# Spreading the first triangular inverse of a delta-rule kernel by four row masks instead of two, with a share of it on GpSimd

## The chip, the cores and the metric

The kernel runs on one core of one Trainium2 chip. The metric is the device time of one execution in microseconds (us). The kernel before takes 661.8 us, the median of 3 runs (661.51 to 662.65). One execution more was taken with the hardware profiler on; all instants below are counted from the start of its span.

## The reference, cut to what matters

Two blocks follow each other. The first is a delta rule over 4 batches x 8 heads, 768 steps, head size 48:

```python
k_n = k / (np.linalg.norm(k, axis=-1, keepdims=True) + 1e-06)
for t in range(S):
    kt, vt, bt = (k_n[:, :, t], v[:, :, t], beta[:, :, t, None])
    y[:, :, t] = np.einsum('bhd,bhde->bhe', q[:, :, t], state)
    v_old = np.einsum('bhde,bhd->bhe', state, kt)
    state = state + bt[:, :, :, None] * np.einsum('bhd,bhe->bhde', kt, vt - v_old)
```

The second is a SwiGLU feed-forward block on its output, 3072 tokens of 384 values, with 1536 hidden units:

```python
g = x @ w_gate
silu = g * (1.0 / (1.0 + np.exp(-g)))
val = x @ w_val
return (silu * val @ w_out)
```

## The kernel before, in words

**Chunks.** The 768 steps are cut into 12 chunks of C = 64 steps. Inside a chunk the recurrence is a triangular system: with A the lower part of the keys' Gram matrix, scaled by beta, the chunk needs Z = (1 + A)^-1. Two chunks form a group. 32 matrices (two chunks x 16, the 16 being "heads of a batch pair") of a group lie side by side in the lanes of VectorE. For the groups after the first, Z is made in 32 x 32 blocks; for the first group, which nothing can hide, it is made in 16 x 16 blocks only (B16 = 16, R = 32), and the parts below these blocks are brought in by matmuls.

**The first group, around the change.**
- `first_tiles` (line 606) clears the place of Z (`first_of["zb"]`, 1056 columns) and makes row masks from the identity: each `tensor_reduce` (line 619) sums some columns of it in both halves, so that a mask is 1 in certain partitions of each half of 64 and 0 elsewhere. `m_rows` holds four masks (rows from 16 on, from 32 on, from 48 on, and below 32), `m_low` the first three negated.
- `first_gram` (line 635) makes the Gram matrices in PSUM, chunk 0 in `px`, chunk 1 in the feed-forward banks 2 and 3. `first_diag` (line 645) puts their blocks on the diagonal into a tile; ScalarE does this for one half of the rows (line 650), VectorE adds the other (line 654). A transposition on VectorE (line 1950) turns "steps in partitions" into "matrices in partitions".
- `low_copies` (line 663) is six ScalarE instructions for a chunk (line 667): they copy the part of the Gram matrix below the blocks from PSUM into `l_sb`, negated and masked.
- `first_scale` (line 673) scales the blocks by beta over the squared norm; GpSimd writes that factor onto Z's diagonal (line 676), VectorE scales both blocks whole (line 680).
- `first_substitution` (line 689) is 15 steps of two VectorE instructions, a product (line 700) and a sum (line 706).
- `first_z` (line 708) transposes Z back on VectorE (line 710): 1024 columns, in rows of 32, of which half hold the 16 x 16 blocks' second half for the other mask.
- `spread_z` (line 713) writes Z into `ztp[0]`, where it serves as the weights of matmuls: one mask for the upper 32 rows, one for the lower 32. For chunk 0 it is four instructions of 256 columns, one on ScalarE (line 723) and three on VectorE (line 725); for chunk 1 it is one of 512 columns on each of the two.
- `n_products` (line 727) multiplies Z and the lower part: 64 matmuls of 64 x 64 (line 733) for a chunk, into banks 2 and 3. It needs all of `spread_z` for its chunk and all of `low_copies`. `first_advance` (line 940) begins with it, and its other products (line 952) follow, each on the one before, until x of chunk 0 is there (lines 1040 and 1041) and the feed-forward matmuls begin (line 1562).
- `unread` (line 630) is a filler: matmuls of a constant whose result nobody reads (line 633).

**What sets the order.** All five engines are under a manual schedule: each executes its instructions in the order in which the program text issues them, and waits in that order. So the end of the start phase is written out by hand at lines 1930 to 1990.

**The weights** come in pieces (`pieces`, numbered n). `stage(n, after)` (line 253) starts the DMA of a piece on SyncE's queue (line 262). With `after` given, GpSimd first copies one column from the staged piece `after` into the place of piece n (line 261): GpSimd thus waits until that earlier piece has landed, and SyncE waits for GpSimd, so that only a few pieces are on the way at once. Pieces 0 to 5 are staged right after `first_scale`, pieces 2 to 5 with `after` = 0 to 3. Later in GpSimd's order come the two halves of a mask on the products of q and k of chunk 0 (`under_mask`, line 537) and then the copies for pieces 6, 7 and so on.

Of the kernel before, what the change touches and what calls it, by code (L numbers as in the profile page):

```python
# [20 lines left out]
def kernel(  # L21
# [25 lines left out]
    nc = tc.nc  # L47
# [4 lines left out]
    NB = B // 2  # L52
# [5 lines left out]
    HH = NB * H  # L58
# [3 lines left out]
    const = ctx.enter_context(tc.tile_pool(name="const", bufs=1))  # L62
# [60 lines left out]
    ztp = [const.tile([128, 2, HH, C], FP32, name=f"zt{i}") for i in range(ZB)]  # L123
# [55 lines left out]
    def load_v(c):  # L179
        vin[c] = work.tile([128, 2, NB, NJ, D], FP32, name="vin", bufs=2)  # L180
        for b in range(2):
            src = halves(v, c, b).rearrange("bp (j par) p d -> par p (bp j) d", par=2)
            for par in range(2):
                s = half_of(b ^ par if c > 1 else b).start
                nc.sync.dma_start(  # L185
                    out=vin[c][s : s + 64, par].rearrange("p bp j d -> p (bp j) d"),
                    in_=src[par],
                )
# [28 lines left out]
    staged, powers, places = {}, {}, {}  # L217

    def words(tile_):
# [3 lines left out]
    places = {  # L223
        "z0": zt_flat[0],
        "z1": zt_flat[1],
        "wo": words(wo_sb).rearrange("p t d -> p (t d)"),
    }
    H_ = PIECE
# [12 lines left out]
    for n, (name, lo) in enumerate(place_of):  # L241
        m = 2 * pieces[n][4]
# [7 lines left out]
        at = max(before) if before else LATE.get(name, -1)  # L250
# [78 lines left out]
    for b in range(2):  # L329
        rows = mask_q[64 * b : 64 * b + 64]  # L330
        nc.gpsimd.affine_select(
            out=rows,
# [5 lines left out]
            channel_multiplier=-1,  # L338
        )

    m_rows = const.tile([128, 4], FP32, name="m_rows")
    m_low = const.tile([128, 3], FP32, name="m_low")
    m_two = const.tile([128, 4, 2], FP32, name="m_two")

    p_places = [const.tile([128, 1024], FP32, name=f"p_sb{i}") for i in range(2)]
    spent, late_loads = [], []
# [105 lines left out]
    def banks(name, tag):  # L452

        if type(tag) is int:
            return [ps_ffn([128, 512], name, tag + i) for i in range(2)]
        p = ps_pair(name, tag)
        return [p[:, 0], p[:, 1]]
# [100 lines left out]
    def new_mb():  # L558
        return work.tile([128, R, R], FP32, name="mb", bufs=1)
# [38 lines left out]
    first_of, l_sb, n_sb = {}, {}, {}  # L598
    B16 = R // 2

    def pairs_of_blocks(flat):

        v = flat.rearrange("p (b n) -> p b n", b=2)[:, :, 0 : B16 * R]
        return v.rearrange("p b (k i) -> p b k i", i=R)

    def first_tiles():
        a = work.tile([128, C * 2 * HH], FP32, name="a_sb")
        for c in range(2):
            l_sb[c] = a[:, R * R * c : R * R * (c + 1)].rearrange(
                "p (h k) -> p h k", k=C  # L610
            )
        first_of["flat"] = new_mb().rearrange("p k i -> p (k i)")
        first_of["zb"] = places["z1"].bitcast(FP32)[:, 4 * H_ - 1056 : 4 * H_]
        first_of["mb"] = places["wo"].bitcast(FP32)[:, 2 * H_ : 2 * H_ + 1056]
        nc.vector.memset(first_of["zb"], 0.0)
        for c in range(2):
            nc.vector.memset(l_sb[c][:, :, 48:C], 0.0)
        for x, rows in enumerate((slice(16, C), slice(R, C), slice(48, C), slice(0, R))):
            nc.vector.tensor_reduce(
                out=m_two[:, x],  # L620
                in_=ident.rearrange("p (b n) -> p b n", b=2)[:, :, rows],
                axis=mybir.AxisListType.X,
                op=ALU.add,
            )
        nc.vector.tensor_tensor(
            out=m_rows, in0=m_two[:, :, 0], in1=m_two[:, :, 1], op=ALU.add
        )
        nc.vector.tensor_scalar_mul(m_low, m_rows[:, 0:3], -1.0)

    def unread(count, p, m=512):  # L630

        for _ in range(count):
            nc.tensor.matmul(p[0:R, 0:m], half, half[:, 0:1].to_broadcast([128, m]))
# [11 lines left out]
    def first_diag(c, p, between=None):  # L645
        to = first_of["flat"].rearrange("p (j c par h) -> p c par j h", c=2, par=2, j=R)
        to = to[:, c]
        p = [p_h.rearrange("p x h j -> p x j h") for p_h in p]
        for par in range(2):
            nc.scalar.mul(to[:, par], p[par][:, 0], m_rows[:, 3:4])  # L650
            if between and par == 0:
                between()
        for par in range(2):
            nc.vector.scalar_tensor_tensor(
                out=to[:, par],
                in0=p[par][:, 1],
                scalar=m_rows[:, 1:2],
                in1=to[:, par],
                op0=ALU.mult,
                op1=ALU.add,  # L660
            )

    def low_copies(c, p):
        l_v = l_sb[c].rearrange("p (par h) k -> p par h k", par=2)
        for par in range(2):
            for x in range(3):
                nc.scalar.mul(
                    l_v[:, par, :, B16 * x : B16 * x + B16],
                    p[par][:, x // 2, :, B16 * (x % 2) : B16 * (x % 2) + B16],
                    m_low[:, x : x + 1],  # L670
                )

    def first_scale(r_b):
        zb, b = first_of["zb"], beta_b[:, 0]
        nc.vector.tensor_tensor(out=b, in0=b, in1=r_b, op=ALU.mult)
        nc.gpsimd.tensor_copy(zb[:, 0 : R * R : R + 1], b)
        mb = pairs_of_blocks(first_of["mb"])[:, :, :, 0:B16]
        for x in range(2):
            at = slice(B16 * x, B16 * x + B16)
            nc.vector.scalar_tensor_tensor(  # L680
                out=mb[:, x],
                in0=mb[:, x],
                scalar=-1.0,
                in1=b[:, None, at].to_broadcast([128, B16, B16]),
                op0=ALU.mult,
                op1=ALU.mult,
            )

    def first_substitution():

        zb, mb = pairs_of_blocks(first_of["zb"]), pairs_of_blocks(first_of["mb"])
        for j in range(B16 - 1):
            m = B16 - 1 - j
            shape = [128, 2, m, j + 1]
            t_v = tmp_of[nc.vector][:, 0 : 2 * (j + 1) * m].rearrange(
                "p (b i k) -> p b i k", b=2, i=m
            )
            z_v = zb[:, :, j + 1 : B16, 0 : j + 1]
            m_v = mb[:, :, j : j + 1, j + 1 : B16].rearrange("p b o i -> p b i o")
            nc.vector.tensor_tensor(  # L700
                out=t_v,
                in0=zb[:, :, j : j + 1, 0 : j + 1].to_broadcast(shape),
                in1=m_v.to_broadcast(shape),
                op=ALU.mult,
            )
            nc.vector.tensor_tensor(out=z_v, in0=z_v, in1=t_v, op=ALU.add)

    def first_z():
        z = new_mb().rearrange("p k i -> p (k i)")
        nc.vector.transpose(z, first_of["zb"][:, 0 : R * R])  # L710
        first_of["z"] = z.rearrange("p (i m) -> p i m", i=R)

    def spread_z(c, x, engine, bps=slice(0, NB)):

        def by_bp(t):
            t = t.rearrange("p (par bp j) i -> p par bp j i", par=2, bp=NB)[:, :, bps]
            return t.rearrange("p par bp j i -> p par (bp j) i")

        z_v = by_bp(first_of["z"].rearrange("p i (c h) -> p c h i", c=2)[:, c])
        out = by_bp(ztp[0][:, c, :, R * x : R * x + R])  # L720
        mask = m_rows[:, 1:2] if x else m_rows[:, 3:4]
        if engine is nc.scalar:
            nc.scalar.mul(out, z_v, mask)
        else:
            engine.tensor_scalar_mul(out, z_v, mask)

# [213 lines left out]
    def first_advance():  # L940
# [5 lines left out]
        to = nc.vector.tensor_copy  # L946
# [15 lines left out]
        t = x_flat.rearrange("p (x bp j d) -> p x bp j d", x=3, bp=NB, j=NJ)  # L962
# [41 lines left out]
        for bp in range(NB):  # L1004
# [6 lines left out]
            )  # L1011
            plus(uu[:, :, bp], t[:, 1:3, bp], pairs[bp])
        spread_z(1, 0, nc.vector)
        held_loads[26] = lambda: load_v(2)
        yield
        pq = p_sb.pop(0)
# [25 lines left out]
            if bp == 0:  # L1042
                unread(1, banks("p_t", 0)[1], 256)
        unread(1, banks("p_t", 0)[1], 256)
        spread_z(1, 1, nc.scalar)
        yield
        p_s = of_state(0, uu)
        nc.scalar.copy(state, p_s)
# [870 lines left out]
    with tc.manual_schedule(  # L1919
# [22 lines left out]
        p_g = [first_gram(0, "px")]  # L1942
# [3 lines left out]
        spread_beta(copy_a)  # L1946
        turned(0, True, 0)
        low_copies(0, p_g[0])
        low_copies(1, p_g[1])
        nc.vector.transpose(first_of["mb"][:, 0 : R * R], first_of["flat"])  # L1950
        r_b = first_n()
        first_scale(r_b)
# [11 lines left out]
        first_q.append(gram_steps(1, True, "px", (copy_a, copy_a)))  # L1964
        next(first_q[1])
        next(first_q[0])
        unread(4, banks("p_t", 2)[0])
        first_substitution()
        first_z()
        some, others = slice(0, 1), slice(1, NB)  # L1970
        spread_z(0, 1, nc.scalar, some)
        spread_z(0, 0, nc.vector, some)
        spread_z(0, 0, nc.vector, others)
        spread_z(0, 1, nc.vector, others)
        scale_v(0)
        next(first_q[1])
        next(first_q[0])
# [129 lines left out]
```

## Time and profile before

| what | value |
|---|---|
| median of 3 runs | 661.8 us |
| the profiled execution's own time | 663.32 us |
| its span, first to last instruction | 661.6 us |
| TensorE (PE) busy | 649.8 us, 98% |
| VectorE (DVE) busy | 475.0 us, 72% |
| ScalarE (ACT) busy | 281.3 us, 43% |
| GpSimd (POOL) busy | 198.7 us, 30% |
| last VectorE instruction of the substitution ends | 24.86 us |
| first matmul of `n_products(0)` | 28.80 us |
| first feed-forward matmul (line 1562) | 41.75 us |

In a row of the timeline the columns are: start (us), duration from the first to the last of the row's instructions (us), engine, line of the kernel, operation, output<-input by the program's names, shapes, count; in brackets the idle time of the engine just before and what ended it. PE is TensorE's matmuls, PEld its weight loads; SPq is SyncE's DMA queue. A tile that lies in a place borrowed from another has that one's name: Z during the substitution is "zt", its scaled blocks are "wo_sb", and Z after the transposition back is "mb". In the table by stretches, "1.67 (x81)" is 1.67 us busy in 81 instructions, and PEclk is the granted TensorE clock, 1.00 being full speed.

### The profile page before, as it was taken

To read this page: it belongs to the slowest core of one execution; us is meant where nothing else is said; L and a number is where in the kernel's file an instruction comes from. 1 tells how busy PE (TensorE), PEld (TensorE's weight loads), DVE (VectorE), ACT (ScalarE), POOL (GpSimd) and SP (SyncE) were. 2 spreads that over 40 slices of the span, in tenths; PEclk is the share of its full clock that TensorE was granted. 3 is DMA by queue.
4 is the path that set the end of the run, shared out by engine and by line. 5 is a ranking of instruction groups with operands and counts; after the bars stand their busy time and mean duration, and the time that the engine had idled before them with its cause. 6 is when DMAs were issued, how large, how long until landed. Compare 5 with 4: busy or idle time off the path is not lost.

```text
span 661.6 us, 24916 instructions
## 1 busy us (share of the span) xinstructions
PE 649.8 (98%) x10854; PEld 596.5 (90%) x10854; DVE 475.0 (72%) x989; ACT 281.3 (43%) x626; POOL 198.7 (30%) x312
## 2 busy tenths in 40 slices
PE   8989999999999999999999999999999999999997
PEld 4667888767999999999999999999999999999997
DVE  6779699999689767758667758667758655655563
ACT  4887757224435433434532533532433432333230
POOL 8030041013894032880031881030882000000000
PEclk8989999999999999999999999999999999999999
DMA  9659763005742451364464264364263442232220
GB/s 138 144 165 265 214 145 119 1 14 92 201 78 73 97 122 51 84 142 89 99 127 92 61 152 104 81 131 105 62 142 88 93 109 67 58 97 65 81 72 25
DMA packets 147438, 68.57 MB, mean 104 GB/s; under 512 B 123456, under 2 KB 126560, under 8 KB 147328
## 3 DMA queue, kind: packets, MB, share of 16 engines
q1 hardware_dynamic: 144832, 66.28, 42.8%
q8 instruction: 85, 1.39, 0.9%
q10 hardware_dynamic: 2240, 0.59, 0.5%
q0 software_dynamic: 256, 0.10, 0.2%
q14 instruction: 25, 0.20, 0.1%
HBM read 59.08 MB, written 7.86 MB: 101 GB/s over the span
## 4 chain that ended last, share of the span: by engine, by line
PE 86%; DVE 7%; SPq 3%; issue 2%; DMA 1%; ACT 1%; POOL 0%; DVEq 0%; ACTq 0%; POOLq 0%
PE ffn L1405 39%; PE ffn L1682 21%; PE ffn L1562 9%; PE ffn L1591 2%; SPq L139 2%; PE p_px L1167 2%; PE p_py L498 1%; DVE x_t L583 1%; DVE zb L589 1%; PE p_px L921 1%; PE p_py L1069 1%; PE p_py L1086 1%; PE p_px L1150 1%; PE p_px L498 1%; SPq L185 1%
## 5 line engine op out<-in xcount | busy, mean ns | idle before, releaser
L1405 PE MATMUL ffn<-x_t,w_gv 128*128 128x128 f32 x800 | 108.7, 279 | 0.9 <-DVE p_sb L1632 0.8
L1405 PEld LDWEIGHTS ffn<-x_t,w_gv 128*128 128x128 f32 x800 | 97.4, 192 | 4.1 <-DVE p_sb L1632 2.0
L1439 ACT ACTIVATE sil<-ffn 128x256 f32<-128x256 f32 x100 | 36.4, 383 | 115.3 <-PE ffn L1405 108.0
L1405 PE MATMUL ffn<-x_ffn,w_gv 128*128 128x128 f32 x640 | 84.6, 275 | 0.0
L1682 PE MATMUL ffn<-wo_sb,h_f 128*128 128x192 f32 x480 | 83.9, 328 | 0.0
L1682 PEld LDWEIGHTS ffn<-wo_sb,h_f 128*128 128x128 f32 x480 | 77.9, 190 | 0.6
L1405 PEld LDWEIGHTS ffn<-x_ffn,w_gv 128*128 128x128 f32 x640 | 78.0, 192 | 0.3
L820 POOL TENSOR_TENSOR n_b<-mb,half 128x32 f32<-128x32 f32 x5 | 27.9, 5582 | 161.4 <-DVE mb L552 161.4
L583 POOL TENSOR_TENSOR h_f<-zb,mb 128x31 f32<-128x31 f32 (+15 forms) x124 | 69.4, 559 | 19.2 <-PE p_py L798 6.0
L589 POOL TENSOR_TENSOR zb<-zb,h_f 128x31 f32<-128x31 f32 (+15 forms) x124 | 70.8, 571 | 9.7
L1405 PE MATMUL ffn<-x_t,h_f 128*128 128x128 f32 x472 | 64.7, 280 | 0.0
L1405 PEld LDWEIGHTS ffn<-x_t,h_f 128*128 128x128 f32 x472 | 57.3, 192 | 1.6 <-DVE ffn L1632 0.5
L1440 DVE TENSOR_TENSOR h_f<-sil,ffn 128x256 f32<-128x256 f32 x100 | 39.3, 418 | 24.0 <-ACT sil L1439 24.0
L1101 ACT COPY x_ffn<-p_py 32x256 f32<-32x256 f32 (+3 forms) x108 | 39.4, 365 | 29.0 <-PE p_py L1086 27.3
L1632 DVE TENSOR_TENSOR ffn<-p_sb,ffn 128x512 f32<-128x512 f32 x40 | 27.8, 696 | 25.9 <-PE ffn L1405 25.2
L1635 DVE TENSOR_TENSOR ffn<-ffn,p_sb 128x512 f32<-128x512 f32 x40 | 27.5, 691 | 19.9 <-PE ffn L1405 19.0
L1682 PE MATMUL ffn<-last_k,h_f 128*128 128x192 f32 x200 | 36.0, 327 | 0.0
L1635 DVE TENSOR_TENSOR o_sb<-o_sb,ffn 128x192 f32<-128x192 f32 x50 | 17.5, 350 | 24.2 <-PE ffn L1682 23.5
L1562 PE MATMUL ffn<-x_t,w_gv 128*128 128x256 f32 x144 | 33.9, 385 | 0.2 <-DVE x_t L1041 0.2
L1682 PEld LDWEIGHTS ffn<-last_k,h_f 128*128 128x128 f32 x200 | 32.9, 190 | 0.1
L1562 PE MATMUL ffn<-x_ffn,w_gv 128*128 128x256 f32 x144 | 31.9, 380 | 0.0
L1405 PE MATMUL ffn<-x_ffn,h_f 128*128 128x128 f32 x232 | 30.9, 276 | 0.0
(330 smaller groups left out, 1171.8 us busy)
## 6 DMA issues: line engine op xcount, KB each, us to landing
h_f<-w_s SPq DMA_DIRECT2D x81, 256.0 KB, 2.8
more_w<-w_s SPq DMA_DIRECT2D x27, 256.0 KB, 2.7
vin<-in_v_dram SPq DMA_DIRECT2D x48, 96.0 KB, 3.5
out_dram<-o_sb SPq DMA_DIRECT2D x46, 96.0 KB, 2.2
kn<-in_k_dram SPq DMA_DIRECT2D x20, 192.0 KB, 4.5
zt<-in_moe_w_out_dram SPq DMA_DIRECT2D x10, 384.0 KB, 4.2
qpad<-in_q_dram SPq DMA_DIRECT2D x36, 64.0 KB, 3.0
w_s<-h_f SPq DMA_DIRECT2D x7, 256.0 KB, 2.6
```

The costliest lines, as they stand in the source:

```text
L139: dmas[b % len(dmas)].dma_start(out=t[64 * b : 64 * b + 64, :, :, 0:D].rearrange("p bp h d -> p (bp h) d"), in_=halves(x, c, b).rearrange( ...
L583: engine.tensor_tensor(out=t_v, in0=zb[:, 0 : j + 1, j : j + 1].to_broadcast([128, j + 1, m]), in1=mb[:, j : j + 1, j + 1 : R].to_broadcas ...
L589: engine.tensor_tensor(out=zb[:, 0 : j + 1, j + 1 : R], in0=zb[:, 0 : j + 1, j + 1 : R], in1=t_v, op=ALU.add,)
L820: nc.gpsimd.tensor_tensor(out=n, in0=mb.rearrange("p j i -> p (j i)")[:, 0 : R * R : R + 1], in1=half, op=ALU.pow,)
L1101: nc.scalar.copy(x_all[at % 128 : at % 128 + rows, at // 128].rearrange("p (bp b i) -> p bp b i", bp=NB, b=2), p[64 * half + lo : 64 * hal ...
L1405: nc.tensor.matmul(p[:, u], w(u), moving, start=start and u == 0, stop=True, skip_group_check=True,)
L1439: nc.scalar.activation(silu_of, p[:, 0:2], ACTF.Silu)
L1440: nc.vector.tensor_tensor(out=h_of(c, PAIRS[r][e % 3], e // 3), in0=silu_of, in1=p[:, 2:4], op=ALU.mult)
L1562: nc.tensor.matmul(ps[name][:, i], w_sb[:, t, (f + i) * 128 : (f + i + 1) * 128], xts[c][:, t], start=(t == 0 and i == 0), stop=(t == KT - 1),
L1632: nc.vector.tensor_tensor(out=out, in0=a, in1=b, op=ALU.subtract)
L1635: nc.vector.tensor_tensor(out=out, in0=a, in1=b, op=ALU.add)
L1682: nc.tensor.matmul(p[x, part], a(f - f % 2)[:, f % 2], b(f), start=not begun and f == 0, stop=f == FH - 1, skip_group_check=True,)
```

## The change

Z's two 16 x 16 blocks now lie side by side in rows of 32, so that the transposition back has 512 columns instead of 1024. Spreading then takes four masks of 16 rows each instead of two of 32: four instructions of 256 columns for each chunk. For chunk 0 one is on ScalarE, one on GpSimd and two on VectorE; for chunk 1 two on VectorE and two on ScalarE. In `first_scale`, the factor is written to the diagonal by VectorE, only the entries above the diagonal are scaled, rows 0 to 3 by VectorE and rows 4 to 14 by GpSimd; the sign that this product had is now in the masks of `first_diag`. `low_copies(1)` is moved from behind `low_copies(0)` to just ahead of the last fillers, and these write to `py` instead of bank 2. Three masks are added.

```diff
-        for x, rows in enumerate((slice(16, C), slice(R, C), slice(48, C), slice(0, R))):
+        starts = (slice(16, C), slice(R, C), slice(48, C), slice(0, R))
+        quarters = [slice(B16 * x, B16 * x + B16) for x in range(3)]
+        for x, rows in enumerate(list(starts) + quarters):
...
-        first_of["zb"] = places["z1"].bitcast(FP32)[:, 4 * H_ - 1056 : 4 * H_]
+        first_of["zb"] = places["z1"].bitcast(FP32)[:, 4 * H_ - 528 : 4 * H_]
...
-        nc.gpsimd.tensor_copy(zb[:, 0 : R * R : R + 1], b)
-        mb = pairs_of_blocks(first_of["mb"])[:, :, :, 0:B16]
-        for x in range(2):
-            at = slice(B16 * x, B16 * x + B16)
-            nc.vector.scalar_tensor_tensor(
-                out=mb[:, x],
-                in0=mb[:, x],
-                scalar=-1.0,
-                in1=b[:, None, at].to_broadcast([128, B16, B16]),
-                op0=ALU.mult,
-                op1=ALU.mult,
-            )
+        diag = zb[:, 0 : B16 * (R + 1)].rearrange("p (i n) -> p n i", i=B16)
+        b_v = b.rearrange("p (x i) -> p x i", x=2)
+        nc.vector.tensor_copy(diag[:, 0 : B16 + 1 : B16], b_v)
+        mb = pairs_of_blocks(first_of["mb"])
+        for engine, js in ((nc.vector, slice(0, 4)), (nc.gpsimd, slice(4, B16 - 1))):
+            m = mb[:, :, js, js.start + 1 : B16]
+            in1 = b_v[:, :, None, js.start + 1 : B16].to_broadcast(list(m.shape))
+            engine.tensor_tensor(out=m, in0=m, in1=in1, op=ALU.mult)
...
-        z = new_mb().rearrange("p k i -> p (k i)")
-        nc.vector.transpose(z, first_of["zb"][:, 0 : R * R])
-        first_of["z"] = z.rearrange("p (i m) -> p i m", i=R)
+        z = new_mb().rearrange("p k i -> p (k i)")[:, 0 : B16 * R]
+        nc.vector.transpose(z, first_of["zb"][:, 0 : B16 * R])
+        first_of["z"] = z.rearrange("p (i c h) -> p c h i", i=B16, c=2)
...
+    def spread_z(c, y, engine):
+
+        z_v = first_of["z"][:, c]
+        out = ztp[0][:, c, :, B16 * y : B16 * y + B16]
+        mask = m_rows[:, 4 + y : 5 + y] if y < 3 else m_rows[:, 2:3]
         if engine is nc.scalar:
             nc.scalar.mul(out, z_v, mask)
+        elif engine is nc.gpsimd:
+            mask = mask[:, :, None].to_broadcast([128, HH, B16])
+            engine.tensor_tensor(out=out, in0=z_v, in1=mask, op=ALU.mult)
         else:
             engine.tensor_scalar_mul(out, z_v, mask)
...
         spread_z(1, 0, nc.vector)
+        spread_z(1, 1, nc.vector)
...
-        spread_z(1, 1, nc.scalar)
+        spread_z(1, 2, nc.scalar)
+        spread_z(1, 3, nc.scalar)
...
         low_copies(0, p_g[0])
-        low_copies(1, p_g[1])
         nc.vector.transpose(first_of["mb"][:, 0 : R * R], first_of["flat"])
         r_b = first_n()
         first_scale(r_b)
         load_v(1)
         for n in range(6):
             stage(n, n - 2 if n > 1 else None)
...
         next(first_q[1])
         next(first_q[0])
-        unread(4, banks("p_t", 2)[0])
+        low_copies(1, p_g[1])
+        unread(4, banks("p_t", "py")[0])
         first_substitution()
         first_z()
-        some, others = slice(0, 1), slice(1, NB)
-        spread_z(0, 1, nc.scalar, some)
-        spread_z(0, 0, nc.vector, some)
-        spread_z(0, 0, nc.vector, others)
-        spread_z(0, 1, nc.vector, others)
+        spread_z(0, 3, nc.scalar)
+        spread_z(0, 2, nc.gpsimd)
+        spread_z(0, 0, nc.vector)
+        spread_z(0, 1, nc.vector)
         scale_v(0)
```

More of the change, by code (lines that the diff above doesn't have):

```diff
@@ L339 @@
         )
-    m_rows = const.tile([128, 4], FP32, name="m_rows")
-    m_low = const.tile([128, 3], FP32, name="m_low")
-    m_two = const.tile([128, 4, 2], FP32, name="m_two")
+    m_rows = const.tile([128, 7], FP32, name="m_rows")
+    m_low = const.tile([128, 4], FP32, name="m_low")
+    m_two = const.tile([128, 7, 2], FP32, name="m_two")
     p_places = [const.tile([128, 1024], FP32, name=f"p_sb{i}") for i in range(2)]
@@ L627, in first_tiles @@
         )
-        nc.vector.tensor_scalar_mul(m_low, m_rows[:, 0:3], -1.0)
+        nc.vector.tensor_scalar_mul(m_low, m_rows[:, 0:4], -1.0)
     def unread(count, p, m=512):
@@ L649, in first_diag @@
         for par in range(2):
-            nc.scalar.mul(to[:, par], p[par][:, 0], m_rows[:, 3:4])
+            nc.scalar.mul(to[:, par], p[par][:, 0], m_low[:, 3:4])
             if between and par == 0:
@@ L656, in first_diag @@
                 in0=p[par][:, 1],
-                scalar=m_rows[:, 1:2],
+                scalar=m_low[:, 1:2],
                 in1=to[:, par],
@@ L675, in first_scale @@
         nc.vector.tensor_tensor(out=b, in0=b, in1=r_b, op=ALU.mult)
-        nc.gpsimd.tensor_copy(zb[:, 0 : R * R : R + 1], b)
-        mb = pairs_of_blocks(first_of["mb"])[:, :, :, 0:B16]
-        for x in range(2):
-            at = slice(B16 * x, B16 * x + B16)
-            nc.vector.scalar_tensor_tensor(
-                out=mb[:, x],
-                in0=mb[:, x],
-                scalar=-1.0,
-                in1=b[:, None, at].to_broadcast([128, B16, B16]),
-                op0=ALU.mult,
-                op1=ALU.mult,
-            )
+        diag = zb[:, 0 : B16 * (R + 1)].rearrange("p (i n) -> p n i", i=B16)
[6 more added lines that the diff above has]
+            engine.tensor_tensor(out=m, in0=m, in1=in1, op=ALU.mult)
     def first_substitution():
-        zb, mb = pairs_of_blocks(first_of["zb"]), pairs_of_blocks(first_of["mb"])
+        zb = first_of["zb"][:, 0 : B16 * R].rearrange("p (i x k) -> p x i k", x=2, k=B16)
+        mb = pairs_of_blocks(first_of["mb"])
         for j in range(B16 - 1):
@@ L708, in first_z @@
     def first_z():
-        z = new_mb().rearrange("p k i -> p (k i)")
-        nc.vector.transpose(z, first_of["zb"][:, 0 : R * R])
-        first_of["z"] = z.rearrange("p (i m) -> p i m", i=R)
[L713 to L721, printed above, removed]
+        z = new_mb().rearrange("p k i -> p (k i)")[:, 0 : B16 * R]
[5 more added lines that the diff above has]
+        mask = m_rows[:, 4 + y : 5 + y] if y < 3 else m_rows[:, 2:3]
         if engine is nc.scalar:
             nc.scalar.mul(out, z_v, mask)
+        elif engine is nc.gpsimd:
+            mask = mask[:, :, None].to_broadcast([128, HH, B16])
+            engine.tensor_tensor(out=out, in0=z_v, in1=mask, op=ALU.mult)
         else:
```

## The prediction, on record before the result

> **What bounds the kernel now.** I read the shares of busy time first, then TensorE by stretches, then the timeline of each engine around the change.
>
> ```profile
> PE 649.8 (98%) x10854; PEld 596.5 (90%) x10854; DVE 475.0 (72%) x989; ACT 281.3 (43%) x626; POOL 198.7 (30%) x312
> ```
>
> ```profile
> 41.75:50.00 8.25, 7.63 (x209) 6.13 (x210) 6.57 (x18) 8.19 (x22) 2.22 (x6) 1.00 0.68 206
> 50.00:60.00 10.00, 10.00 (x282) 8.38 (x281) 9.86 (x33) 7.96 (x22) 0.34 (x1) 1.00 0.99 236
> 60.00:70.00 10.00, 9.07 (x228) 7.50 (x221) 8.52 (x21) 6.34 (x16) 0.00 (x0) 1.00 1.02 341
> 70.00:80.00 10.00, 10.00 (x51) 8.84 (x50) 7.41 (x16) 7.49 (x11) 0.00 (x0) 1.00 0.82 199
> ```
>
> The columns are the stretch and its length, then the busy time of TensorE, its weight loads, VectorE, ScalarE and GpSimd, the granted clock, and the DMA share and rate. From 41.75 us on, where the feed-forward matmuls begin, TensorE has almost no idle time: 0.62 us in the first stretch, 0.93 us in the third. So whatever moves the first feed-forward matmul moves the end by nearly as much. Ahead of it TensorE is busy too, but with fillers:
>
> ```profile
> 24.15 1.16 PE L498 MATMUL p_px<-qt,kt 64*64 64x64 f32 x64
> 25.24 3.63 PE L633 MATMUL ffn<-half 128*32 128x512 f32 x8
> 28.80 1.16 PE L733 MATMUL ffn<-zt,a_sb 64*64 64x64 f32 x64
> ```
>
> Line 633 is the filler, line 733 is `n_products(0)`. From there to 41.75 is a chain of products, each waiting for the copy of the one before. What `n_products(0)` needs is ready earlier than 28.80:
>
> ```profile
> 24.90 1.25 DVE L710 STREAM_TRANSPOSE mb<-zt 128x1024 f32<-128x1024 f32 x1
> 26.18 1.15 DVE L725 TENSOR_SCALAR zt<-mb,m_rows 128x256 f32<-128x256 f32 x3
> 27.23 0.96 DVE L450 TENSOR_TENSOR vin<-vin,n_t 128x768 f32<-128x768 f32 x1
> ```
>
> VectorE's three spreads end at 27.33, ScalarE's one (26.18, 0.75 long) at 26.93. TensorE takes its instructions in order, so the fillers, not Z, end last, by 1.5 us. The view that decides is GpSimd's timeline:
>
> ```profile
> 15.40 0.50 POOL L676 COPY zt<-beta_b 128x32 f32<-128x32 f32 x1 [1.00 <-DVE beta_b L675]
> 25.96 0.19 POOL L261 COPY h_f<-h_f 128x1 uint32<-128x1 uint32 x1 [10.06 <-DMA h_f<-in_moe_w_gate_dram]
> 27.95 0.29 POOL L261 COPY h_f<-h_f 128x1 uint32<-128x1 uint32 x1 [1.80 <-DMA h_f<-in_moe_w_val_dram]
> 28.89 0.18 POOL L261 COPY h_f<-h_f 128x1 uint32<-128x1 uint32 x1 [0.65 <-DMA h_f<-in_moe_w_gate_dram]
> 32.10 0.18 POOL L261 COPY h_f<-h_f 128x1 uint32<-128x1 uint32 x1 [3.02 <-DMA h_f<-in_moe_w_val_dram]
> 32.24 2.77 POOL L537 TENSOR_TENSOR p_sb<-p_sb,mask_q 128x512 f32<-128x512 f32 x2
> 34.95 0.25 POOL L261 COPY h_f<-h_f 128x1 uint32<-128x1 uint32 x1
> ```
>
> The four copies of line 261 are those of `stage` for pieces 2 to 5; each waits until an earlier weight piece has landed. GpSimd keeps the order of the text: the mask of line 537 reads products that ScalarE had copied by 26.14 (25.05 + 1.09), and it still starts at 32.24, right behind the fourth copy. The new `spread_z(0, 2, nc.gpsimd)` stands in the text between that copy and this mask.
>
> **The change part by part.**
>
> *Masks and clearing.* The clearing took 0.94 us for 1056 columns; 528 cost about 0.5 (272 columns took 0.285). Three more reductions cost 0.13 each, as the four did (2.55 to 3.09). The two cancel, and SyncE's queue, which waits for the last of these VectorE instructions (3.48 + 0.29), starts as before, within 0.1 us.
>
> *`low_copies(1)` moved.* It leaves ScalarE at 17.21 (six instructions, 1.71 us) and stands behind the two copies of line 518 (before: 25.05 to 26.14). ScalarE's copies ahead of it come earlier, but TensorE's own sequence lies between them, so I give 0.4 us of the 1.71. Then `low_copies(1)` runs to about 27.4 and the spread on ScalarE (0.75) to about 28.2. Nothing for TensorE. If that cover were gone, ScalarE would be late by up to 1.3 us (28.2 against 26.93).
>
> *Fillers to `py`.* The same eight matmuls, 3.63 us. They now wait for the two copies of line 523 out of `py` (24.09 + 1.07 = 25.16); before they began at 25.24. Nothing, or 0.4 us earlier.
>
> *`first_scale`.* Out go two VectorE instructions (0.77 us together); in come one of 120 elements (0.28, as line 700 at 128x120) and the diagonal, not shown before; the rows of 128x32 on VectorE say 0.17 to 0.19. VectorE gains 0.3. GpSimd gets 242 elements, 0.63 to 0.70 us (lines 583 and 589 at 128x240), from about 15.4; substitution step 4 is the first to read them, some 2 us later. The Trainium skill (SBUF — State Buffer, "Who interferes with whom") speaks against it: a VectorE instruction with two SBUF inputs and a GpSimd one that reads SBUF lock each other out. The row agrees as far as it goes: GpSimd's 128x32 copy took 0.50 us here beside VectorE and 0.378 on average in line 564. By that rule VectorE's gain would be lost and 0.4 us more; it would stay off the path.
>
> *Transposition and spreads of chunk 0.* 1024 to 512 columns: half of 1.25 is 0.62, while 128x512 rows elsewhere (line 552) say 1.17; I take 0.6 saved (0.1 at least). VectorE's spreads go from three to two: 0.38 saved. VectorE is thus done at about 26.0 instead of 27.33. None of it is on the path, because of the next item.
>
> *The quarter on GpSimd.* It starts in line 537's place, at 32.24. Its length, 256 elements with a broadcast mask: 0.73 (line 589, 128x256), 0.65 (line 583), 0.70 (half of line 537's 1.40); I take 0.73, with bounds 0.6 and 1.4. It ends at 32.97; the step from one engine to the next takes 0.05 elsewhere (VectorE's end at 34.21, TensorE's start at 34.27). `n_products(0)` starts at 33.02 instead of 28.80: **+4.2 us**. The waiting matmul has the whole of TensorE's chain behind it, ScalarE's and VectorE's copies behind that, and the conversion of weights that stands between them in their orders. Bounds of this term: +3.2 if piece 1's landing (5.0 us after its issue, piece 0's 3.6) were a microsecond quicker, +5 with the 1.4.
>
> *Behind it on GpSimd and SyncE.* The masks of line 537 end 0.73 later, at about 35.7; they are read at 36.69 before, some 41 after. The copies for pieces 6 and 7, and their DMAs (issued at 35.23 and 35.69), come up to 0.8 later, their readers 4 or 5 later. Nothing.
>
> *TensorE's clock.* The fillers end at 28.4 to 28.9, and TensorE then idles more than 4 us, with no filler left. What a slack stretch does here (length, TensorE busy, granted clock, DMA):
>
> ```profile
> 34.00:37.00 3.00, 1.67 (x81) 0.98 0.34 98
> 37.00:40.00 3.00, 2.79 (x63) 0.50 0.33 118
> 40.00:43.00 3.00, 2.81 (x12) 0.95 0.75 234
> ```
>
> In finer stretches the half clock lasts from 36.85 to 40.3, after 3 us at little over half load. Its price: the pair of products at 36.69 takes 1.83 us (to 38.52), the same pair at 29.78 took 1.11; three transpositions 0.90 against 0.55; fillers 0.96 against 0.62. That is 1.4 us for 3.4 us of half clock. After an idle time of over 4 us I expect one such stretch more, on `n_products(0)` and the first pair of products: 0.7 to 1.5, and I take **+1.0**. It may be nothing (the old stretch only moves) or twice. The Trainium skill (TensorE: Matmul & The Clock Gate, Part 1) has the clock halved after a whole idle window of about 3.4 us and restored after a busy one; the length agrees with 3.4 here, the cause not quite, as TensorE was not idle in the 3 us ahead. By that rule alone there would be one or two such stretches.
>
> *Chunk 1.* VectorE: two of 0.44 in place of one of 0.66, ahead of 1.0 us of idle time. ScalarE: two of 0.75 in place of 1.18, +0.3, where it is full (8.19 of 8.25 us) but TensorE has feed-forward work. I take 0, with 0.3 as the upper end.
>
> **The sum** against the profiled execution: +4.2 + 1.0 = +5.2 us, so its span goes from 661.6 to 666.8, its own time from 663.3 to 668.5. The median of the runs shown, 661.8, lies 1.5 under that time; it goes to **667.0 us**.
>
> **The rivals.**
>
> *No gate on GpSimd (not slower).* If GpSimd came to its spread before the fillers end, that is if its fourth copy ended by 28.0 instead of 32.28, then the earlier sequence on TensorE would show and nothing else: 0.4 us less, 661.4, or 661.8 if VectorE and GpSimd hinder each other. It decides on whether the spread is really queued behind the landing of piece 3. For it speaks only that the new trace may order GpSimd otherwise; against it, line 537's start at 32.24 with its data there at 26.14. Chance 0.07.
>
> *The delay is absorbed later.* Weights get 4 us of lead; if TensorE's idle time after 41.75 (0.62 + 0.93, and 0.4 of small waits) came from them and vanished, and the half clock cost only what it costs now, less 1.4 where the old stretch goes: 5.2 - 1.9 - 1.4 = +1.9, 663.7. Against it: that idle time has no weight as its releaser. Chance 0.07.
>
> *Two more stretches of half clock.* Nearly 7 us at half speed cover `n_products(0)` and three pairs: +2.6 in place of 1.0, so 668.6. For it: the chain's load in 31 to 34 was 2.51 of 3 at full clock, not dense. Chance 0.13.
>
> **The numbers.** The forecast as summed has 0.73. Its own range: gate +3.2 to +5, clock 0 to 1.5, chunk 1 up to 0.3, seldom all at one end: 664.8 to 668.3. The range for 8 in 10 leaves out the two low rivals and takes in most of the third: 664.4 to 668.9. About 0.2% (1.3 us) is what a measurement of this kernel tells from no change. Faster by more: 0.02, the far tail of the first rival. Within: 0.08, most of it and part of the second. Slower: 0.90.
>
> **What would show it.** GpSimd: a spread of 128x256 right behind the fourth copy of line 261's kind, at about 32.2. TensorE: idle from about 28.6 to 33.0, its wait ended by GpSimd; PEclk 0.50 somewhere in 32 to 37; the first feed-forward matmul near 47. VectorE's two spreads done near 26, ScalarE's near 28, both unused. The prediction is wrong if GpSimd's spread starts before 28, or if TensorE's idle time after the first feed-forward matmul shrinks by as much as that start is late.

## The result, and the profile after

The changed kernel takes 666.94 us, the median of 6 runs (665.54 to 668.16), beside 662.22 us for the kernel before (6 runs, 661.36 to 664.01): a ratio of 1.0052, 95% interval 1.0032 to 1.0072. The profiled execution's span went from 661.6 to 666.2 us. Against another set of runs (`e5_changed_again` below) the ratio was 1.0054 (1.0033 to 1.0075).

First the shares of busy time and TensorE by stretches, now from 46.5 us on, with the columns as before:

```profile
PE 649.7 (98%) x10854; PEld 597.3 (90%) x10854; DVE 474.1 (71%) x992; ACT 281.2 (42%) x627; POOL 201.4 (30%) x313
```

```profile
46.50:55.00 8.50, 7.99 (x207) 5.91 (x205) 6.15 (x17) 7.55 (x20) 0.87 (x3) 0.85 0.73 229
55.00:65.00 10.00, 10.00 (x223) 8.37 (x222) 9.72 (x30) 7.84 (x20) 0.00 (x0) 1.00 0.75 174
65.00:75.00 10.00, 10.00 (x284) 8.52 (x284) 9.41 (x23) 7.35 (x19) 0.00 (x0) 1.00 0.73 241
```

TensorE has the same work. The stretch that had 0.93 us of idle time is now full; the first still has 0.51, and it runs in part at half clock (0.85). The 0.93 us were two stops for which no engine is named, 0.74 us among the matmuls of line 1194 (a later product of the delta rule) and 0.19 us in line 921. The larger one, in the kernel before:

```profile
62.75 1.01 PE L1194 MATMUL p_px<-v,zb 64*64 64x48 f32 x51 [0.74 <-issue]
```

GpSimd's timeline shows where the wait arises:

```profile
15.41 0.71 POOL L685 TENSOR_TENSOR wo_sb<-wo_sb,beta_b 128x242 f32<-128x242 f32 x1 [1.01 <-DVE beta_b L677]
26.35 1.26 POOL L261 COPY h_f<-h_f 128x1 uint32<-128x1 uint32 x2 [10.22 <-DMA h_f<-in_moe_w_gate_dram]
30.30 0.18 POOL L261 COPY h_f<-h_f 128x1 uint32<-128x1 uint32 x1 [2.69 <-DMA h_f<-in_moe_w_gate_dram]
30.96 0.18 POOL L261 COPY h_f<-h_f 128x1 uint32<-128x1 uint32 x1 [0.48 <-DMA h_f<-in_moe_w_val_dram]
31.10 0.75 POOL L721 TENSOR_TENSOR zt<-mb,m_rows 128x256 f32<-128x256 f32 x1
31.81 2.50 POOL L537 TENSOR_TENSOR p_sb<-p_sb,mask_q 128x512 f32<-128x512 f32 x2
```

The spread (line 721 of the changed kernel) stands where the prediction put it, behind the fourth staging copy and ahead of the mask of line 537. Z itself had been ready for 5 us by then. TensorE's fillers and its wait (line 731 is `n_products` now):

```profile
24.18 3.63 PE L635 MATMUL p_py<-half 128*32 128x512 f32 x8
31.91 1.94 PE L731 MATMUL ffn<-zt,a_sb 64*64 64x64 f32 x64 [4.09 <-POOL zt L721]
```

The bracket names the wait: 4.09 us of idle time, ended by GpSimd's write of `zt`. The matmuls then take 1.94 us instead of 1.16. The clock says why (length, TensorE busy, granted clock, DMA):

```profile
31.00:34.00 3.00, 2.09 (x80) 0.67 0.52 180
34.00:37.00 3.00, 2.69 (x123) 0.76 0.49 137
37.00:40.00 3.00, 1.48 (x72) 1.00 0.46 132
40.00:43.00 3.00, 2.28 (x117) 0.88 0.77 242
43.00:46.00 3.00, 2.79 (x22) 0.50 0.51 150
```

In finer stretches, half clock goes from 32.0 to 35.4 us and again from 42.3 to 49.1. The first feed-forward matmul comes at 47.20 instead of 41.75 us. VectorE's part behaved as meant in one place and not in the other:

```profile
15.46 0.81 DVE L685 TENSOR_TENSOR wo_sb<-wo_sb,beta_b 128x120 f32<-128x120 f32 x1
25.04 0.71 DVE L709 STREAM_TRANSPOSE mb<-zt 128x512 f32<-128x512 f32 x1
25.78 0.79 DVE L723 TENSOR_SCALAR zt<-mb,m_rows 128x256 f32<-128x256 f32 x2
```

The transposition takes 0.71 instead of 1.25 and the spreads 0.79 instead of 1.15, but the 120 elements that were to take 0.28 took 0.81.

### The profile page after: what moved, and what is told of

It reads as the page before. It is cut to its first block, busy times and chain, and to the rows that moved or that the text cites. A ratio compares the mean times of both kernels' runs of the same rounds, so it can differ in the third digit from the quotient of the medians.

```text
span 666.2 us, 24921 instructions
## 1 busy us (share of the span) xinstructions
PE 649.7 (98%) x10854; PEld 597.3 (90%) x10854; DVE 474.1 (71%) x992; ACT 281.2 (42%) x627; POOL 201.4 (30%) x313
## 4 chain that ended last, share of the span: by engine, by line
PE 86%; DVE 7%; SPq 3%; issue 2%; ACT 1%; DMA 1%; POOL 0%; DVEq 0%; ACTq 0%
PE ffn L1405 40%; PE ffn L1682 21%; PE ffn L1562 9%; PE ffn L1591 2%; SPq L139 2%; PE p_px L1167 2%; PE p_py L498 1%; DVE x_t L583 1%; DVE zb L589 1%; PE p_py L1069 1%; PE p_px L919 1%; PE p_py L1086 1%; PE p_px L1150 1%; PE p_px L498 1%; SPq L185 1%
## 5 line engine op out<-in xcount | busy, mean ns | idle before, releaser
L1405 PEld LDWEIGHTS ffn<-x_t,w_gv 128*128 128x128 f32 x800 | 97.4, 192 | 3.9 <-DVE p_sb L1632 1.8
L818 POOL TENSOR_TENSOR n_b<-mb,half 128x32 f32<-128x32 f32 x5 | 30.4, 6087 | 166.8 <-DVE mb L552 166.8
L1635 DVE TENSOR_TENSOR ffn<-ffn,p_sb 128x512 f32<-128x512 f32 x40 | 27.5, 691 | 20.3 <-PE ffn L1405 19.5
L1562 PEld LDWEIGHTS ffn<-x_t,w_gv 128*128 128x128 f32 x144 | 27.2, 195 | 4.7 <-ACT w_gv L274 0.8
```

Of the source, the lines that this page charges most:

```text
L818: nc.gpsimd.tensor_tensor(out=n, in0=mb.rearrange("p j i -> p (j i)")[:, 0 : R * R : R + 1], in1=half, op=ALU.pow,)
L1405: nc.tensor.matmul(p[:, u], w(u), moving, start=start and u == 0, stop=True, skip_group_check=True,)
L1562: nc.tensor.matmul(ps[name][:, i], w_sb[:, t, (f + i) * 128 : (f + i + 1) * 128], xts[c][:, t], start=(t == 0 and i == 0), stop=(t == KT - 1),
L1635: nc.vector.tensor_tensor(out=out, in0=a, in1=b, op=ALU.add)
```

## The experiments

My theory: the quarter on GpSimd waits behind copies that wait for weights, and the idle time costs clock besides. The rival: something else in the change costs the time. Each ratio below is to the kernel before, run on the same chip in the same set. "Half clock" is worked out for each execution from its span and mean granted clock, as span x (1 - clock) x 2, and averaged over the runs of a kernel.

**Does the quarter on GpSimd do it?** The changed kernel with that quarter on VectorE:

```diff
-        spread_z(0, 2, nc.gpsimd)
+        spread_z(0, 2, nc.vector)
```

> The changed kernel, but the quarter of chunk 0 that GpSimd spreads is spread by VectorE, as a third instruction there. My theory (the quarter waits on GpSimd behind the staging copies): VectorE's three spreads end near 27.0 us, ScalarE's near 27.3, the fillers near 27.8, so n_products(0) starts near 27.8 instead of 31.91 and with no half clock ahead of it; 661 to 662 us, at or a little under the kernel before. Rival (something else in the change costs the time: the moved copies on ScalarE, the scaling on GpSimd, the spreads of chunk 1): still 665 or more.

662.90 us, ratio 0.9993 (0.9972 to 1.0014). The whole loss is gone with this one line, and the rival with it. But there is no gain either, although `n_products(0)` starts 1.45 us earlier than in the kernel before. TensorE's waits show what took its place (the last line is the kernel before):

```profile
27.35 1.30 PE L731 MATMUL ffn<-zt,a_sb 64*64 64x64 f32 x61 [0.47 <-DVE zt L723]
29.82 0.33 PE L950 MATMUL p_px<-v,qpad 64*64 64x48 f32 x8 [0.18 <-ACT v L975]
32.39 0.88 PE L950 MATMUL p_px<-v,qpad 64*64 64x48 f32 x22 [2.24 <-issue]
```

```profile
31.69 0.51 PE L952 MATMUL p_px<-v,qpad 64*64 64x48 f32 x21 [0.28 <-issue]
```

After eight matmuls of the second product TensorE stops for 2.24 us, and no engine is named. In the kernel before the same stop, after the same eight matmuls, is 0.28 us (it goes on at 31.69). What was won at the start is lost there, and with 10.2 us of half clock from 32.1 us on some more: the first feed-forward matmul comes at 43.57 us, against 41.75 before.

**Is it GpSimd, or its place in the queue?** The changed kernel with the staging of pieces 3 to 5 behind the spread:

```diff
-        for n in range(6):
+        for n in range(3):
             stage(n, n - 2 if n > 1 else None)
...
         spread_z(0, 2, nc.gpsimd)
+        for n in range(3, 6):
+            stage(n, n - 2)
```

> The changed kernel with the quarter still on GpSimd, but the staging copies and DMAs of weight pieces 3 to 5 issued behind it instead of ahead, so that only the copy for piece 2 stands ahead. My theory (the place in GpSimd's queue costs, not GpSimd as such): the quarter starts at 26 to 26.6 us, n_products(0) near 27.8; 661 to 662.5 us, the pieces 3 to 5 landing at most 1 us later without a reader that waits. Rival (an instruction on GpSimd is slow or late to release TensorE wherever it stands): 665 or more.

664.18 us, ratio 1.0013 (0.9990 to 1.0035): most of the loss is gone with the quarter still on GpSimd, though the time came out above the expected 662.5. GpSimd in this run:

```profile
27.15 0.34 POOL L261 COPY h_f<-h_f 128x1 uint32<-128x1 uint32 x1 [11.02 <-DMA h_f<-in_moe_w_gate_dram]
27.45 0.74 POOL L721 TENSOR_TENSOR zt<-mb,m_rows 128x256 f32<-128x256 f32 x1
```

The spread is as long as before (0.74) and starts 3.65 us earlier; the copy ahead of it was itself a microsecond later than expected, and `n_products(0)` starts at 28.29 us.

**Is it enough alone?** The kernel before with one spread of chunk 0 on GpSimd:

```diff
+        elif engine is nc.gpsimd:
+            mask = mask[:, :, None, None].to_broadcast(list(out.shape))
+            engine.tensor_tensor(out=out, in0=z_v, in1=mask, op=ALU.mult)
...
-        spread_z(0, 1, nc.vector, others)
+        spread_z(0, 1, nc.gpsimd, others)
```

> The kernel before with one thing changed: its last spread of chunk 0 (256 columns, on VectorE) is on GpSimd. My theory: this alone gives the loss; the spread starts behind the fourth staging copy at 31 to 32.3 us, n_products(0) 0.8 later, half clock after it, 665 to 668 us. Rival (the loss needs the other parts of the change): under 663.5.

667.48 us, ratio 1.0074 (1.0049 to 1.0100): the loss, without any other part of the change. Half of `n_products(0)`, which does not need that spread, ran at 28.09; the other half:

```profile
33.39 1.14 PE L736 MATMUL ffn<-zt,a_sb 64*64 64x64 f32 x32 [4.60 <-POOL zt L726]
```

**What is the half clock worth?** First, fillers over the wait (changed kernel, alone and again beside it):

```diff
-        unread(4, banks("p_t", "py")[0])
+        unread(8, banks("p_t", "py")[0])
```

> The changed kernel with eight unread products in place of four ahead of n_products(0), so that TensorE is busy until about 31.4 us while it waits for GpSimd. My theory (about 1 us of the loss is half clock that the idle time brings on): n_products(0) starts as before near 31.9 but takes 1.16 us instead of 1.94, PEclk 1.00 there; 0.7 to 1.5 us less than the changed kernel, 665.4 to 666.2 us. Rival (the half clock is only moved, the wait is all of the loss): within 0.4 us of the changed kernel.

> The changed kernel once more, as the measure for the others on the same chip. 666 to 668 us, between 0.4% and 0.8% over the kernel before. On average 8 us of half clock in an execution against some 5 in the kernel before.

> The changed kernel with eight unread products in place of four, beside the changed kernel on one chip. Theory A (the fillers keep the clock up and that is worth something): 0.4 to 1.2 us under the changed kernel, with 1 to 3 us less half clock on average. Theory B (what is gained in clock is lost, since the wait for GpSimd still sets the start and half clock comes later instead): within 0.4 us of it.

`e4_more_fillers` took 668.33 us, ratio 1.0074 (1.0045 to 1.0102), no gain; in its profile `n_products(0)` did run in 1.16 us. Side by side: the changed kernel 667.67, ratio 1.0054 (1.0033 to 1.0075); with the fillers 668.32, ratio 1.0066 (1.0041 to 1.0091), and in this profile `n_products(0)` took 1.99 us. Half clock fell from 12.0 us on average (8 were expected) to 5.3, and the time did not. The first expectation failed, its rival too. Of the third, theory A failed; the 0.65 us between the medians is above the 0.4 of theory B, within the noise, and half clock did not come later instead.

In the profiles the gate moved: the fourth staging copy comes at 32.48 us (31.94 in `e4_more_fillers`) against 30.82 in `e5_changed_again`, and `n_products(0)` at 33.42 (32.88) against 31.77. But the later gate is not what kept the gain away. The chain behind it was shorter, and the first feed-forward matmul came at 46.63 us (45.55), against 46.77 in `e5_changed_again` and 47.20 in the first profile of the changed kernel. The loss stands further back, in line 1194, where TensorE stops with no engine named; first `e5_changed_again`, then `e6_more_fillers_again`:

```profile
61.08 0.72 PE L1194 MATMUL p_px<-v,zb 64*64 64x48 f32 x33 [0.17 <-issue]
```

```profile
62.27 0.84 PE L1194 MATMUL p_px<-v,zb 64*64 64x48 f32 x41 [2.30 <-issue]
```

In `e4_more_fillers` this stop is 1.74 us, in the first profile of the changed kernel there is none of 0.15 us or more. The profile of `e6_more_fillers_again` has half clock from 63.1 to 66.5 us behind it besides. So these runs do not say what the half clock at the start is worth by itself.

The other way round, the kernel before without the time of its fillers, but with as many instructions:

```diff
-        unread(4, banks("p_t", 2)[0])
+        unread(4, banks("p_t", 2)[0], 16)
```

> The kernel before with its four unread products ahead of n_products(0) cut from 512 to 16 columns: as many instructions, 3.3 us less time. If the fillers and not Z end last, as the prediction has it, n_products(0) starts at 27.3 to 27.6 us instead of 28.8, right behind VectorE's last spread. What that is worth: 0.5 to 1.4 us if half clock stays as it is; nothing, or up to 1 us more than the kernel before, if the idle time ahead brings half clock on, at about 0.3 us for each us of it, or if the fetch of instructions still lands when it did.

664.50 us, ratio 1.0020 (0.9996 to 1.0044). `n_products(0)` starts 1.7 us earlier, at the end of ScalarE's spread, so the fillers did end last:

```profile
27.07 1.16 PE L733 MATMUL ffn<-zt,a_sb 64*64 64x64 f32 x64 [2.14 <-ACT zt L723]
```

Half clock rose to 11.8 us, from 4.6 in the kernel before. Over the runs of the kernel before, three sets of 27, 35 and 29, a straight line of time against half clock rises 0.26, 0.29 and 0.30 us for each us (correlation 0.81, 0.69, 0.70). At 0.3, the 7.2 us more would cost 2.2 us, and with 1.7 us won at the start 0.5 us of loss would be left; the medians differ by 1.55. The profile shows that the start was not worth its 1.7 us: the first feed-forward matmul comes at 42.10 us, 0.35 later than before, behind half clock from 28.4 to 31.8 us and again from 38.7, and stops in the products. The fillers do not lose by ending last.

**What is the stop without a name, and what moved the gate?** The stop has a place: from the eighth matmul of the second product to the eighth of the fourth there are 128 matmuls and as many weight loads. The profile's page of the kernel before counts, by packets, MB and share of the DMA engines:

```profile
q8 instruction: 85, 1.39, 0.9%
```

That is 16.4 KB a packet, or 64 bytes for each of 256 instructions; and the trace has 21,866 instructions of TensorE (its matmuls, its weight loads and 158 more), which is 85.4 times 256. I took it that TensorE waits there for its instructions, and moved the border with six small fillers:

```diff
+        unread(6, banks("p_t", "py")[0], 16)
         unread(4, banks("p_t", "py")[0])
```

> The changed kernel with its GpSimd quarter on VectorE, and six unread products of 16 columns ahead of the four large ones: 12 more matmuls and 12 more weight loads, under 0.6 us. Theory A (with the quarter on VectorE, TensorE's next stop is the fetch of its instructions: it stands after the same matmul of the second product in every trace, until 1.3 us after a block of instructions has landed): the small fillers move the border of the blocks into the fillers, the block is asked for some 2 us earlier, no stop with releaser issue is left in the first and third product on n_sb, and the time is 1 to 2 us under the run with the quarter on VectorE alone, 660.5 to 661.8 us, under the kernel before. Theory B (the stop is something else, or the fetch finds another place to hinder): 662 to 663.5 us, as the kernel before.

> The kernel before with the same six small unread products ahead of its four. Theory A (instruction fetch stops TensorE for 0.28 and 0.54 us in the products): both stops go, n_products(0) starts up to 0.5 us later, so 0 to 0.8 us less than the kernel before. Theory B: no change or up to 0.5 us more.

On the version with the quarter on VectorE 664.26 us, ratio 1.0010 (0.9983 to 1.0037); on the kernel before 664.67 us, ratio 1.0010 (0.9986 to 1.0034). Theory A was right about the place and wrong about the gain. On the kernel before the first stop went and the second grew from 0.54 to 0.87 us. On the other version the stop moved by the 12 matmuls that were put ahead, into the last matmuls of the first product:

```profile
30.75 0.26 PE L950 MATMUL p_py<-vin,zt 64*64 64x48 f32 x2 [0.52 <-issue]
```

but it did not vanish, and three more follow, 0.60 us before 34.48, 1.10 before 39.43 and, in line 1194, 2.31 before 59.61. A border at the start of the fillers did no better:

```diff
-        unread(4, banks("p_t", "py")[0])
+        unread(12, banks("p_t", "py")[0], 16)
+        unread(3, banks("p_t", "py")[0])
```

> The changed kernel with its quarter on VectorE, with twelve unread products of 16 columns and three large ones ahead of n_products(0): 40 more TensorE instructions. The border of the instruction blocks then lies at the start of the fillers, the block is asked for near 24.5 us, before the weight pieces 2 and 3 are on the way, and the first stop with releaser issue should be gone or under 0.3 us. If the stops are what holds this version back: 660.5 to 662 us, 0.1% to 0.3% under the kernel before. If the next fetches take over: 662 to 664 us, no change.

> The changed kernel with its quarter on VectorE once more, as the measure for the others on one chip: within 0.2% of the kernel before, 662 to 664 us; n_products(0) near 27.5 us, a stop with releaser issue of 1 to 2.5 us in the second product.

665.14 us, ratio 1.0026 (1.0008 to 1.0044), above both ranges that were given, with a stop of 0.78 us inside the fillers and one of 0.86 at 34.94; the version without it 662.88 us, ratio 1.0006 (0.9982 to 1.0029). In the latter's profile `n_products(0)` starts at 28.27 us, later than the 27.5 expected, and the stop is 0.99 us. So no version here beats the kernel before: the one with the quarter on VectorE could not be told from it in two sets of runs.

For the gate, 16 small instructions more in the changed kernel:

```diff
+        unread(4, banks("p_t", "py")[0], 16)
         unread(4, banks("p_t", "py")[0])
```

> The changed kernel with four unread products of 16 columns added ahead of its four: 16 more TensorE instructions, some 0.3 us, as many instructions as the eight large ones had added. Theory A (more instructions ahead of n_products(0) pull the fetch of the next block from 33 us to about 28, between the weight pieces that GpSimd waits for, and these land later): the fourth staging copy at 31.5 to 32.7 instead of 30.8 to 31.0, n_products(0) at 32.3 to 33.5; 668 to 669 us. Theory B (landing varies by itself): as the changed kernel, 667 to 667.8 us, with the copy at 31.

671.05 us, ratio 1.0106 (1.0074 to 1.0139), more than either theory said. In its profile the fourth copy comes at 31.90 us and `n_products(0)` at 32.84, as theory A had them. But as with the eight fillers the first feed-forward matmul, at 46.62 us, is no later than in the changed kernel, and the stops stand behind it, 0.98 us in line 731 and 2.38 in line 1194 (`e5_changed_again`: 0.62 and 0.17). The trace's packets of the instruction queue, set beside the fourth copy:

| kernel | instruction packet near the gate starts | fourth staging copy starts |
|---|---|---|
| changed; again | 33.40; 33.32 | 30.96; 30.82 |
| quarter on VectorE; again | 29.84; 28.84 | 30.25; 32.73 |
| before | 29.47 | 32.10 |
| before, one spread on GpSimd | 28.10 | 32.45 |
| changed, eight fillers; again | 27.93; 28.14 | 31.94; 32.48 |
| changed, four small fillers more | 28.25 | 31.90 |
| before, no fillers; small fillers | 28.24; 28.06 | 32.45; 32.73 |
| quarter on VectorE, small fillers; early border | 28.45; 28.75 | 31.07; 31.99 |

Where the packet starts after 29.8 us, the copy is there by 31.0; where earlier, at 31.07 to 32.73. Two profiles of one kernel, the quarter on VectorE, fall on both sides. That the instruction packet delays the weights is thus a relation over 13 profiles (the run with the staging behind the spread is left out), not shown as a cause: what the packets do to each other on their way wasn't tried. In the changed kernel it may be the other way round: its packet starts at 33.40 us, after the gate has opened.

## Why the prediction was right, point by point

**The gate** was right in mechanism and place; its size was off. `n_products(0)` starts 3.1 us later, not 4.2. The spread's 0.75 (0.73 foretold) and the 0.06 to TensorE fit; the term that was mis-sized is the landing of piece 3, taken over from the profile of before (copy at 32.10) while it came at 30.96. The stated lower bound, 3.2 with a quicker landing, was about met, but only half in the way it named: piece 1 had landed 0.5 us earlier (its copy at 27.43 for 27.95), and the rest is piece 3 itself. In the changed kernel TensorE's packets of instructions start at 22.92 us and then only at 33.40, behind the eighth matmul of `n_products(0)` (32.04); before, one starts at 29.47. That may be why the weights were quicker here; it is not shown.

**The clock** came out near its size, but no run isolates it. From the start of `n_products(0)` to that of the second product the changed kernel takes 3.39 us (31.91 to 35.30), the one before 2.28 (28.80 to 31.08): +1.1. Over runs, half clock is 3.1 us longer in the first set (8.4, with 5.3 in the set of 27 before) and 5.9 in the second (12.0 and 6.1); at 0.3 us each that is +0.9 and +1.8, against +1.0 foretold. The 0.3 is a slope over runs of the kernel before; over the 12 runs of `e5_changed_again` it is 0.13, and the fillers, which took some 6.6 us of half clock away, gained nothing. The rival of two more stretches happened in the profiled execution (10.2 us of half clock from 25 us on, 3.4 before), but cost less than its +2.6: from `n_products(0)` to the first feed-forward matmul it is 15.3 us for 13.0, and 0.7 of that is longer stops. The Trainium skill (TensorE: Matmul & The Clock Gate, Part 1) has the clock halved after an idle window of about 3.4 us. The trace after agrees with it better than the one before: a half-clock stretch of 3.4 us begins at 32.0, behind 4.1 us without a matmul. The later one, from 42.3, again has no idle stretch of that length ahead.

**What was absorbed.** First feed-forward matmul +5.45; the first weight load from `w_gv` for `x_t` in line 1405 (168.8 to 173.6) +4.8, the last one (642.8 to 647.3) +4.5. So nearly a microsecond came back: the 0.93 us of idle time is gone, a part of the second rival, which I had at 0.07 as a whole. That the sum came out (+4.6 of span for +5.2) is in part luck: this and the smaller gate made up for a longer chain, which the prediction did not have. From 35.30 to 47.20 it takes 11.9 us, from 31.08 to 41.75 it took 10.7, with a stop of 1.38 instead of 0.54 us in the fourth product and the second, longer half clock. (The lower end of the prediction's own range, 664.8, is the span of 661.6 plus 3.2; from the median of 661.8, to which the forecast was added, it would be 665.0.)

**Parts at nothing.** In this profile TensorE's sequence came 1.06 us earlier (fillers at 24.18 for 25.24), not 0.4, and ScalarE's spread was done at 27.26, not 28.2; all of it lay under the wait. How much of that is `low_copies(1)` is not shown: over the profiles the fillers begin at 23.1 to 24.7 us where it is moved and at 24.5 to 25.2 where it is not. `first_scale` gained nothing: VectorE's 120 elements ended at 16.27, right after GpSimd's 242 (16.12), and the substitution began at 16.30 for 16.24. Here the rule that the prediction names from the Trainium skill (SBUF — State Buffer, "Who interferes with whom") was the better guide than the row of 0.28: beside GpSimd's instruction VectorE's took 0.81 us and ended 0.15 us after it. VectorE's spreads were done at 26.57, not 26.0, unused all the same. Chunk 1 on ScalarE took 1.36 us for 1.18.

**The first rival**, no gate, is what the runs with the quarter on VectorE show: 0.9993 and 1.0006, no change, as it was priced (661.4 to 661.8). What it did not have is the reason: `n_products(0)` started 1.45 and 0.53 us earlier in the two profiles, and the next stops and half clock took it back (first feed-forward matmul at 43.57 and 42.58, for 41.75).

## What to carry to other kernels

An instruction's cost on an idle engine is set by what stands ahead of it in that engine's order: look for the last waiting instruction there, here a one-column copy that waits for a DMA, and take its end as the start. When a wait is removed from a chain of small matmuls, look at the stops without a releaser behind it; they can be the next bound. Fillers are worth what the clock is worth, here 0.26 to 0.30 us for each us of half clock over the runs of the kernel before. In the changed kernel 16 TensorE instructions more, large or small, came with a stop of 1.7 to 2.4 us some 30 us behind them, and with no gain or a loss; so look at the whole start phase, and not only at the wait that they fill.

## What the runs showed of the hardware that was not expected

TensorE waits for its own instructions. Between 25 and 50 us the profiles show 20 stops of at least 0.15 us with releaser "issue", in ten of the 14 profiles; 19 of them end 1.20 to 1.47 us after an instruction packet of queue q8 has ended (before: packet end 30.39, matmul 31.69; changed: 38.99 and 40.36; quarter on VectorE: 31.11 and 32.39), and they shift with the number of instructions ahead. Counted over all of TensorE's instructions in the trace, each of the 19 matmuls has 193 or 194 more than a multiple of 256 ahead of it, and as many of these packets have ended by then as the multiple says: in the kernel before 1217 (4 x 256 + 193, with four packets ended) and 1473 (5 x 256 + 193, with five). The other one, of 0.16 us, doesn't fit. Along the chain the next packet starts 3.3 to 4.7 us after the one before in the kernel before and in the changed one, and the 128 pairs of a block, two products with their copies, take about as long: so an earlier start of this chain need not end earlier.

The stops of line 1194, between 56 and 64 us, stand at such borders too, and end 1.2 to 1.9 us after the packet. This one line has 0.74 us in the kernel before, none and 0.17 in the changed kernel, 1.01 and 1.17 with the quarter on VectorE, 2.15 with the staging behind the spread, 1.74 to 2.38 in the changed kernel with 16 instructions more ahead, 2.31 with the six small fillers on VectorE's version, and none with the early border. Why the packet comes late there in some versions is open.

Half-clock stretches last 3.4 us or a multiple (6.8 in the changed kernel), and how much of it an execution has goes with the spread from 660 to 668 us among runs of the kernel before (correlation 0.7 to 0.8).
